# A recurrent cell and a gated feed-forward layer: the seven-product form of the up product from the third chunk on, with the second gate on GpSimd

## The chip, the cores and the metric

The kernel runs on one core of a Trainium2 chip. The time is device microseconds (us) of one execution. A core has a matrix engine (TensorE, PE in the profile, with its weight loads PEld), a vector engine (VectorE, DVE), a scalar engine for activations (ScalarE, ACT), GpSimd (POOL) and SyncE (SP), which here issues most transfers. Each engine works through its own queue in order and waits for others by semaphores. PE writes to PSUM, a memory of banks of 128 x 512 float32; GpSimd works in SBUF, the main on-chip memory.

## The reference

Two layers follow each other. The first is a recurrent cell with a matrix state C and a vector state n, for 4 batches of 8 heads, 768 steps, head dimension 40:

```python
for t in range(S):
    m_new = np.maximum(f_gate[:, :, t] + m, i_gate[:, :, t])
    f_stab = np.exp(f_gate[:, :, t] + m - m_new)
    i_stab = np.exp(i_gate[:, :, t] - m_new)
    m = m_new
    C = f_stab[:, :, None, None] * C + i_stab[:, :, None, None] * np.einsum('bhd,bhe->bhde', vt, kt)
    n = f_stab[:, :, None] * n + i_stab[:, :, None] * kt
    h_tilde = np.einsum('bhde,bhe->bhd', C, qt)
    denom = np.maximum(np.abs(nq), 1.0)          # nq = n . q
    y[:, :, t] = o * h_tilde / denom             # o = sigmoid(o_gate)
```

Its output is rearranged to x with 3072 rows of 320. The second layer is

```python
h = x @ w_in            # 320 -> 2048
g = h * np.cos(h)
return g @ w_out        # 2048 -> 320
```

## The kernel before, in words

**Chunks, cells, slots.** The 768 steps are cut into 6 chunks of 128 (NC). In a chunk, one *cell* per batch b computes the recurrence in its parallel form for 8 heads; cells are numbered n = 4 * chunk + b. The feed-forward layer runs one chunk behind: while the cells of chunk c + 1 are computed, the up product, the gate and the down product of chunk c are. The 2048 columns of w_in are taken in 8 *slots* of 256 (f2 = 0 to 7, two halves e of 128), two slots to a cell. So a chunk has 4 cells or 8 slots, and `both_parts(c, b)` writes out the order of one cell and its two slots by hand: all engines' queues are in the order of these calls. The last chunk's slots (c = 5) have no cell beside them.

**A slot.** `Up` multiplies the transposed x (`xT`, `xL`: all 4 batches side by side, 512 columns) by two column blocks of w_in into two PSUM banks (`pup`, a pool of two, so that the next slot needs both free). L724 is the part over 256 of the 320 dimensions, L718 the last 64. x was scaled by 1/(2 pi) when the cell was normalised, so that the cosine is taken as a sine of the distance to the nearest whole number: `near` (ACT, L732, the whole number), `rest` (DVE, L735, the remainder), `sin` (ACT, L740), `gate` (DVE, L744: product times 2 pi times sine) into `g`.

**Two fast products.** Both large products have a seven-product form (Strassen's, in Winograd's variant). The down product uses it from chunk 1 on: `weight_sums` makes sums of blocks of w_out once, `sums(c, k)` makes for each slot four sums of blocks of g on DVE (L880 to L883, 128x128) into a tile S and four on GpSimd (L885 to L888) into tiles D, S and g; `products` yields 12 products of 160 columns a slot (L992), which `down_slot` runs in quotas of 12 to 14, one slot behind; `late_products` runs the 16 that are left of a chunk in slot 1 of the next. `combine_first`, `combine` (slot 0 of the next chunk, L1002 and L1010 to L1020) and `combine_late` (slot 1, L1025 to L1027) add up the four accumulator banks into outputs.

The up product has the seven-product form in `UpFast`, in chunk 5 only (`fast = NC - 1`). `up_weight_sums` puts sums of w_in blocks into the tiles that held the cells' q and k, which are free by then; `x_sums` makes sums of x blocks. `UpFast` runs four products of 256 columns (L790), two ACT copies of the banks into a tile `s` (L798, L799), a filler of two down products (`fill_in`), three more products on top of what is in the banks, and the last dimensions (L806). Additions of parts of `s` follow on GpSimd (L807, L809) and DVE (L808), then on DVE into the bank b0 (L810) and of b1 and `s` into `s` (L812), which frees b1.

**A cell beside the slots.** In the first slot of a cell: `scores` (PE, L539), `weigh` (DVE, L545, needs the decays E), `decay_exponents` and `decay` of the next cell (GpSimd L423, ACT L437), `values` (PE, L565 to L574), `seam` (PE, L676), `normalize_turned` (DVE, L592 to L613), `fade` (GpSimd, L659). In the second: `seam_out` (a transfer of xL issued by ACT, L683), `state` (DVE, L701), `weigh_k` (GpSimd, L442), at its end `turn_blocks` of the next cell (two DVE transposes, L517) and `scale_q` (GpSimd, L521). `sin_next` loads ACT's table for the sine ahead of use (L1208). At the end of chunks 1 to 3, `sigmoid` (L343, L345) prepares the output gate of the chunk after the next.

The functions that the change touches, with the line numbers of the profile:

Of the kernel before, what the change touches and what calls it, by code (L numbers as in the profile page):

```python
# [11 lines left out]
FP = mybir.dt.float32  # L12
# [17 lines left out]
def kernel(  # L30
# [20 lines left out]
    nc = tc.nc  # L51
# [24 lines left out]
    pb = ctx.enter_context(tc.tile_pool(name="pb", bufs=4))  # L76
# [9 lines left out]
    nil = const.tile([128, 128], BF, name="nil")  # L86
# [4 lines left out]
    firsts = p2.tile([128, 4, C], FP, name="first", tag="S")  # L91
# [3 lines left out]
    wall = const.tile([128, HP, C], BF, name="wall")  # L95
# [3 lines left out]
    ident_b = const.tile([128, 128], BF, name="ident_b")  # L99
# [3 lines left out]
    ks2 = [const.tile([128, 2, H, 64], FP, name=f"ks{i}") for i in range(2)]  # L103
    vs2 = [const.tile([128, 2, H, DV], FP, name=f"vs{i}") for i in range(2)]
    for i in range(2):
        nc.gpsimd.memset(ks2[i][:, :, :, D:64], 0.0)
        nc.gpsimd.memset(vs2[i][:, :, :, D:DV], 1.0)
# [8 lines left out]
    WR = 2 * HP * (C // 32) * D  # L116
    raws = {w: [const.tile([128, WR + 32], FP, name=f"{w}r{i}") for i in range(2)] for w in "qk"}
    for w in "qk":
        nc.vector.memset(raws[w][0], 0.0)

    def clear_low():

        for w in "qk":
            for r in (slice(32, 64), slice(64, 128)):
                nc.scalar.copy(out=raws[w][1][r], in_=raws[w][0][r])


# [16 lines left out]
    def bits_in(n, src, pool, width):  # L144
        bits = pool.tile([128, width, 2], I32, name="bits", tag="bits")
        for rows, piece in src:
            nc.sync.dma_start(out=bits[rows, 0:n], in_=piece)
        return bits
# [44 lines left out]
    def weights_in(f):  # L193
        for i in range(NK):
            src = [(slice(32 * a, 32 * a + 32), w_in_bits[D * (NK * a + i):D * (NK * a + i) + 32, ts(f, WP)]) for a in range(HP)]
            yield w_in_sb[:, i, ts(f, WP)], bits_in(WP, src, pb, WP)
        bits = pb.tile([128, WP, 2], I32, name="bits", tag="bits")
        for e in range(2):
            for a in range(2):
                nc.sync.dma_start(out=bits[64 * e:64 * e + 64, ts(a, 128)].rearrange("r n two -> r (n two)"), in_=w_in_last[e, 2 * f + a])  # L200
        yield w_in_l[:, ts(f, 2)].rearrange("p a n -> p (a n)"), bits
# [18 lines left out]
    spare = [raws[w][1][0:BH, x:x + WQ] for w in "qk" for x in (0, WQ)]  # L220
    spare.append(pc.tile([128, 2 * WQ], FP, name="spare", tag="bits")[0:BH, 0:WQ])
# [89 lines left out]
    def ks(n):  # L311
        return ks2[n // 2 % 2][:, n % 2]
# [42 lines left out]
    def load_two(n, which="qkKv"):  # L355
        c, b = divmod(n, B)
        m = n // 2 % 2
        for name, src in (("q", q), ("k", k)):
            if name in which:
                src = src.rearrange("b (p j) (c t a) d -> j c t (b p) (a d)", j=2, a=C // 32, t=32)  # L360
                for j in range(2):
                    for low in range(1 if n < 2 * B else 2):
                        x = 0 if low else 32
                        dst = raws[name][m][64 * j + 32 * low:64 * j + 32 * low + 32, x:x + WR]
                        nc.sync.dma_start(out=dst.rearrange("t (p x) -> t p x", x=C // 32 * D),
                                          in_=src[j, c, :, 4 * b:4 * b + 8])
        for name, dst, src in (("K", ks2[m], k), ("v", vs2[m], v)):
            if name in which:
                src = src.rearrange("b h (c t) d -> c t b h d", t=C)
                nc.sync.dma_start(out=dst[:, :, :, 0:D], in_=src[c, :, b:b + 2])  # L370
# [14 lines left out]
    def load_M(n):  # L385
        c, b = divmod(n, B)
        if n == B - 1:
            E = pb.tile([128, H, C], FP, name="E3", tag="bits")
# [41 lines left out]
    def decay(n):  # L430
# [4 lines left out]
        for h in range(H):  # L435
# [3 lines left out]
    def weigh_k(n):  # L439
        if n < N - B:  # L440
            kw = p2.tile([128, H, 64], FP, name="kw", tag="kw")
            nc.gpsimd.tensor_tensor(out=kw, in0=ks(n), in1=cols(n, 1, 64), op=OP.mult)  # L442
# [27 lines left out]
    def load_blocks(n):  # L470

        c, b = divmod(n, B)
        m, x = n // 2 % 2, n % 2 * (WR // 2)
        for name, src in (("q", q), ("k", k)):
            src = src.rearrange("b (p j) (c t a) d -> j c t (b p) (a d)", j=2, a=C // 32, t=32)
            for j in range(2):
                dst = raws[name][m][64 * j:64 * j + 32, 32 + x:32 + x + WR // 2]
                nc.sync.dma_start(out=dst.rearrange("t (p x) -> t p x", x=C // 32 * D), in_=src[j, c, :, HP * b:HP * b + HP])

    def low_dimensions_of(n):  # L480
        x = 32 + n % 2 * (WR // 2)
        for w in "qk":
            for j in range(2):
                lo, hi = (raws[w][n // 2 % 2][64 * j + y:64 * j + y + 32, x:x + WR // 2].rearrange("t (x d) -> t x d", d=D) for y in (0, 32))
# [17 lines left out]
    def low_dimensions(n):  # L502

        for w in "qk":
            for j in range(2):
                lo, hi = (raws[w][n // 2 % 2][64 * j + x:64 * j + x + 32, 32:32 + WR].rearrange("t (x d) -> t x d", d=D) for x in (0, 32))
                nc.scalar.copy(out=hi[:, :, 0:D - 32], in_=lo[:, :, 32:D])

    def turn_blocks(n, which="qk"):
        m = n // 2 % 2  # L510
        if n not in qkT:
            qkT[n] = [p1.tile([128, HP, C], FP, name=f"t{i}", tag=f"t{i}") for i in range(2)]
        for w in which:
            i = "qk".index(w)
            x = 32 + n % 2 * (WR // 2)
            src = raws[w][m][:, x:x + WR // 2].rearrange("q (p a d) -> q p a d", a=C // 32, d=D)
# [103 lines left out]
    def normalize(n):  # L620
# [8 lines left out]
        t = p1.tile([128, 3 * C], FP, name="yo", tag="db")[:, 0:DM].rearrange("q (h d) -> q h d", h=H)  # L629
# [31 lines left out]
    def seam(n):  # L661
# [9 lines left out]
        if n < N - B:  # L671
            pu = pool.tile([128, HP, DV], FP, name="pu", tag=tag)
            for p in range(HP):
                for j in range(2):
                    h = 2 * p + j
                    nc.tensor.matmul(pu[64 * j:64 * j + D, p], kws[n][:, h, 0:D], vs(n)[:, h], start=True, stop=True)  # L676
# [29 lines left out]
    class Up:  # L706
# [35 lines left out]
        def gate(self, e):  # L742
            g = gp.tile([128, B * C], FP, name="g", tag="g")
            nc.vector.scalar_tensor_tensor(out=g, in0=self.pu[e], scalar=TWO_PI, in1=self.n[e].bitcast(FP),  # L744
                                           op0=OP.mult, op1=OP.mult)
# [5 lines left out]
    fast = NC - 1  # L751
    Sw, Tx = {}, {}

    def up_weight_sums(part):

        tt = nc.gpsimd.tensor_tensor
        if part == 0:
            S1, S2, S4, S3 = Sw.setdefault(0, [raws[w][m][:, 0:NF // 2 * 128].rearrange("p (f n) -> p f n", n=128)
                                               for m in range(2) for w in "qk"])
            tt(out=S1, in0=A21, in1=A22, op=OP.add)  # L760
            tt(out=S2, in0=S1, in1=A11, op=OP.subtract)
        else:
            S1, S2, S4, S3 = Sw[0]
            tt(out=S3, in0=A11, in1=A21, op=OP.subtract)
            tt(out=S4, in0=A12, in1=S2, op=OP.subtract)

# [4 lines left out]
    def x_sums(c):  # L771
        T1, T2, T4 = Tx[c] = pe.tile([128, H, C], FP, name="Tx", tag="E")[:, 0:3 * B // 2].rearrange("p (k b) t -> k p b t", k=3)
# [6 lines left out]
    class UpFast(Up):  # L779


        def __init__(self, c, f2, fill):
# [14 lines left out]
            s = pe.tile([128, H, C], FP, name="Sx", tag="E").rearrange("p (k b) t -> p k (b t)", k=4)  # L797
# [10 lines left out]
            nc.vector.tensor_tensor(out=s[:, 0], in0=s[:, 0], in1=s[:, 3], op=OP.add)  # L808
            nc.gpsimd.tensor_tensor(out=s[:, 3], in0=s[:, 1], in1=s[:, 2], op=OP.add)  # L809
            nc.vector.tensor_tensor(out=b0[:, second], in0=b0[:, second], in1=s[:, 0], op=OP.add)  # L810
            h = s[:, 0:4:3]
            nc.vector.tensor_tensor(out=h, in0=b1.rearrange("p (k n) -> p k n", k=2), in1=h, op=OP.add)  # L812
            self.n = [p3.tile([128, B * C], I32, name="n", tag="n") for _ in range(2)]
            self.h = h

        def near(self, e):
            if e == 0:
                return super().near(e)
# [606 lines left out]
```

## Time and profile before

The median of three runs is 524.11 us (523.25 to 526.92). The profiled execution took 525.5 us.

| | profiled execution |
|---|---|
| time | 525.5 us |
| span of the trace | 523.7 us |
| granted PE clock | 1.000 |
| bytes moved | 57.83 MB, mean 110 GB/s |
| matrix products of the up product, full form (L724) | 146.4 us busy, 320 records of 600 ns |
| its last dimensions (L718) | 45.2 us, 160 records of 641 ns |
| the same in seven products (L790, L806; chunk 5) | 32 + 5 x 16 records of 379 to 389 ns, 32 of 641 ns |
| down products (L992) with S, D, g | 58.4 + 55.1 + 35.4 + 28.7 + 23.6 us |
| waits of GpSimd for gates (L885 <- L744) | 145.2 us in 30 waits |

Times in the profile are us from the span's start unless marked ns; a busy share counts time in which an engine executed, and waiting does not count. A float32 matrix product appears as two records, so `x8` stands for four products. Records of consecutive products overlap, so the mean of a record is longer than the distance of two. The stages are: to 42 us the first four cells and the first weights; from 42 to some 131 us chunk 0's slots with the weights arriving; then chunk 1 to 207.3, chunk 2 to 287.4, chunk 3 to 367.4, chunk 4 to 446.0, chunk 5 to about 514, and the last outputs.

### The profile page before, as it was taken

To read this page: it belongs to the slowest core of one execution; us is meant where nothing else is said; L and a number is where in the kernel's file an instruction comes from. 1 tells how busy PE (TensorE), PEld (TensorE's weight loads), DVE (VectorE), ACT (ScalarE), POOL (GpSimd) and SP (SyncE) were. 2 spreads that over 40 slices of the span, in tenths; PEclk is the share of its full clock that TensorE was granted. 3 is DMA by queue.
4 is the path that set the end of the run, shared out by engine and by line. 5 is a ranking of instruction groups with operands and counts; after the bars stand their busy time and mean duration, and the time that the engine had idled before them with its cause. 6 is when DMAs were issued, how large, how long until landed. Compare 5 with 4: busy or idle time off the path is not lost.

```text
span 523.7 us, 10589 instructions
## 1 busy us (share of the span) xinstructions
PE 504.7 (96%) x3894; PEld 353.0 (67%) x3894; DVE 415.3 (79%) x852; ACT 301.2 (58%) x570; POOL 247.3 (47%) x392
## 2 busy tenths in 40 slices
PE   6999897979999999999999999999999999999996
PEld 4874564545567676676677677667667767787876
DVE  5899998686868878898778888868898868787875
ACT  6899896647656547744537736526836522343541
POOL 7534654442875753543543642642425435435341
PEclk9999999999999999999999999999999999999999
DMA  9989979898849159149159239159220000010001
GB/s 138 211 221 231 260 162 220 179 187 210 166 143 190 56 114 165 41 122 171 52 115 157 51 100 176 44 118 165 42 81 6 2 5 7 2 50 1 1 1 51
DMA packets 100196, 57.83 MB, mean 110 GB/s; under 512 B 62432, under 2 KB 92736, under 8 KB 100144
## 3 DMA queue, kind: packets, MB, share of 16 engines
q1 hardware_dynamic: 96608, 55.48, 49.1%
q10 hardware_dynamic: 3392, 1.49, 1.4%
q8 instruction: 31, 0.51, 0.4%
q14 instruction: 21, 0.17, 0.1%
q0 software_dynamic: 144, 0.18, 0.1%
HBM read 51.71 MB, written 4.11 MB: 107 GB/s over the span
## 4 chain that ended last, share of the span: by engine, by line
PE 67%; DMA 10%; ACT 6%; SPq 5%; DVE 5%; POOL 4%; issue 2%; ACTq 0%; DVEq 0%; POOLq 0%
PE acc L992 24%; PE pup L724 19%; PE pup L718 6%; PE pup L790 5%; PE late L992 3%; DMA xL<-xT 3%; PE ps L539 3%; ACT E L437 2%; PE vt L574 2%; DMA bits<-in_moe_w_in_dram 2%; PE vt L565 2%; PE pup L806 2%; DMA bits<-in_moe_w_out_dram 2%; SPq L353 1%; DMA E<-M_d 1%
## 5 line engine op out<-in xcount | busy, mean ns | idle before, releaser
L724 PE MATMUL pup<-xT,w_in_sb 128*128 128x512 f32 x320 | 146.4, 600 | 3.8 <-DVE g L744 3.6
L732 ACT ACTIVATE n<-pup 128x512 int32<-128x512 f32 x88 | 49.7, 593 | 156.5 <-PE pup L718 87.9
L724 PEld LDWEIGHTS pup<-xT,w_in_sb 128*128 128x128 f32 x320 | 57.7, 189 | 78.6 <-issue 77.0
L885 POOL TENSOR_TENSOR D<-g 128x128 f32<-128x128 f32 x40 | 20.1, 501 | 177.4 <-DVE g L744 145.2
L735 DVE SCALAR_TENSOR_TENSOR n<-pup,n 128x512 f32<-128x512 f32 x88 | 58.1, 687 | 56.2 <-ACT n L732 54.9
L740 ACT ACTIVATE n<-n 128x512 f32<-128x512 f32 x96 | 58.1, 628 | 20.6 <-DVE n L735 11.2
L744 DVE SCALAR_TENSOR_TENSOR g<-pup,n 128x512 f32<-128x512 f32 x88 | 56.8, 684 | 2.6 <-ACT n L740 1.9
L992 PE MATMUL acc<-w_out_sb,g 128*128 128x160 f32 x320 | 58.4, 303 | 0.0
L992 PE MATMUL acc<-T,g 128*128 128x160 f32 x304 | 55.1, 300 | 0.2 <-DVE g L883 0.2
L437 ACT ACTIVATE E<-E,tab 128x128 f32<-128x128 f32 x160 | 49.0, 388 | 4.2 <-POOL E L423 4.0
L992 PEld LDWEIGHTS acc<-w_out_sb,g 128*128 128x128 f32 x320 | 48.1, 190 | 4.4 <-issue 2.7
L718 PE MATMUL pup<-xL,w_in_l 64*128 64x512 f32 x160 | 45.2, 641 | 3.6 <-POOL w_in_l L179 3.6
L992 PEld LDWEIGHTS acc<-T,g 128*128 128x128 f32 x304 | 45.8, 190 | 2.3 <-issue 1.4
L843 PE MATMUL po<-w_out_sb,g 128*128 128x320 f32 x128 | 36.3, 436 | 2.6 <-POOL w_out_sb L179 2.6
L992 PE MATMUL acc<-T,S 128*128 128x160 f32 x160 | 35.4, 303 | 0.0
L843 PEld LDWEIGHTS po<-w_out_sb,g 128*128 128x128 f32 x128 | 23.9, 190 | 14.3 <-POOL w_out_sb L179 3.6
L539 PEld LDWEIGHTS ps<-t,t 40*128 40x128 f32 (+1 forms) x384 | 24.8, 188 | 10.3 <-issue 5.4
L545 DVE TENSOR_TENSOR E<-ps,E 128x512 f32<-128x512 f32 x48 | 30.7, 680 | 0.0
L992 PEld LDWEIGHTS acc<-T,S 128*128 128x128 f32 x160 | 26.1, 190 | 6.0 <-issue 6.0
L992 PE MATMUL acc<-w_out_sb,S 128*128 128x160 f32 x160 | 28.7, 299 | 0.0
L179 POOL TENSOR_TENSOR w_out_sb<-w_out_sb,bits 128x640 int32<-128x640 int32 x8 | 12.6, 1573 | 32.8 <-ACT E L437 14.4
L521 POOL TENSOR_TENSOR qG<-t,G 128x512 f32<-128x512 f32 x20 | 25.4, 1271 | 4.4 <-DVE t L517 4.2
(232 smaller groups left out, 981.4 us busy)
## 6 DMA issues: line engine op xcount, KB each, us to landing
E<-M_d SPq DMA_DIRECT2D x22, 512.0 KB, 3.6
qr<-in_q_dram SPq DMA_DIRECT2D x34, 160.0 KB, 3.2
kr<-in_k_dram SPq DMA_DIRECT2D x34, 160.0 KB, 5.0
bits<-in_moe_w_out_dram SPq DMA_DIRECT2D x8, 640.0 KB, 4.0
G<-G_d SPq DMA_DIRECT2D x18, 256.0 KB
bits<-in_moe_w_in_dram SPq DMA_DIRECT2D x32, 128.0 KB, 4.6
out_dram<-o_sb SPq DMA_DIRECT2D x23, 160.0 KB, 1.9
o<-in_o_gate_dram SPq DMA_DIRECT2D x40, 80.0 KB, 3.2
```

The source lines that it names most:

```text
L437: nc.scalar.activation(out=Es[n][:, h], in_=Es[n][:, h], func=AF.Exp, scale=-1.0, bias=tab[:, c, 0, g:g + 1])
L539: nc.tensor.matmul(ps[j][:, p], kT[r, p], qT[r, p], start=True, stop=True)
L545: nc.vector.tensor_tensor(out=w, in0=pss[n][j], in1=w, op=OP.mult)
L718: nc.tensor.matmul(pu, w_in_l[r, f2], xL[c][r].rearrange("p b t -> p (b t)"), start=ahead, stop=not ahead)
L724: nc.tensor.matmul(pu.rearrange("p (b t) -> p b t", b=B), w_in_sb[:, i, ts(2 * f2 + e, 128)], xT[c][:, i:NK * B:NK], start=(i == 0 and not ...
L732: nc.scalar.activation(out=self.n[e], in_=self.pu[e], func=AF.Copy, bias=0.25)
L735: nc.vector.scalar_tensor_tensor(out=self.n[e].bitcast(FP), in0=self.pu[e], scalar=0.25, in1=self.n[e], op0=OP.add, op1=OP.subtract)
L740: nc.scalar.activation(out=r, in_=r, func=AF.Sin, scale=TWO_PI_DOWN)
L744: nc.vector.scalar_tensor_tensor(out=g, in0=self.pu[e], scalar=TWO_PI, in1=self.n[e].bitcast(FP), op0=OP.mult, op1=OP.mult)
L790: nc.tensor.matmul(bank[:, part].rearrange("p (b t) -> p b t", b=B // 2), w[:, f2], x, start=start, stop=stop, skip_group_check=True)
L843: nc.tensor.matmul(po[c][b], gs[c, f][:, ts(b, C)], w_out_sb[:, f], start=(f == 0), stop=(f == NF - 1))
L992: nc.tensor.matmul(a, lhs, rhs, start=start, stop=stop)
```

## The change

1. `fast` is 2: chunks 2 to 5 use `UpFast`. A new `both_parts_fast` writes out the order of a cell and two slots for them. The decays of the next cell are split: six heads after the sines of the first slot, two (`range(AHEAD, H)`) in the second slot after its copies. `scale_q` moves from the end of the second slot to the start of the next cell; `sums` of the second slot moves behind `turn_blocks`; `seam` becomes the filler of the second slot, and the two down products stay the filler of the first.
2. The second gate (e = 1) of a fast slot goes to GpSimd, whose product has no scalar factor, as does the addition of L808; b1 is added up into `g` itself and freed.
3. The factor 2 pi leaves the gates and is applied when outputs are added up (`add_turns`, and a scale of ACT's copies).
4. `sums` becomes four DVE operations of 128x256 and none on GpSimd, in all chunks.
5. Memory: q and k blocks are loaded a cell at a time (`load_blocks`) into two half-size buffers; one tile `blocks` holds rings for S, D, the weights' bits and `s`; the sums of w_in lie in a tile `room` whose space the first cells' k uses before, and in place of one w_in block. They are made in chunk 1, by three calls in place of two. The copies on ACT that cleared the second q and k buffers at the start are gone.

```diff
-    fast = NC - 1
+    fast = 2
...
-            s = pe.tile([128, H, C], FP, name="Sx", tag="E").rearrange("p (k b) t -> p k (b t)", k=4)
+            s = blocks[:, FREE_AT:FREE_AT + 8].rearrange("p (k b) t -> p k (b t)", k=4)
...
             nc.gpsimd.tensor_tensor(out=s[:, 1], in0=s[:, 1], in1=s[:, 0], op=OP.add)
-            nc.vector.tensor_tensor(out=s[:, 0], in0=s[:, 0], in1=s[:, 3], op=OP.add)
+            nc.gpsimd.tensor_tensor(out=s[:, 0], in0=s[:, 0], in1=s[:, 3], op=OP.add)
             nc.gpsimd.tensor_tensor(out=s[:, 3], in0=s[:, 1], in1=s[:, 2], op=OP.add)
             nc.vector.tensor_tensor(out=b0[:, second], in0=b0[:, second], in1=s[:, 0], op=OP.add)
-            h = s[:, 0:4:3]
-            nc.vector.tensor_tensor(out=h, in0=b1.rearrange("p (k n) -> p k n", k=2), in1=h, op=OP.add)
+            self.g = gp.tile([128, B * C], FP, name="g", tag="g")
+            nc.vector.tensor_tensor(out=self.g.rearrange("p (k n) -> p k n", k=2), in0=b1.rearrange("p (k n) -> p k n", k=2), in1=s[:, 0:4:3], op=OP.add)
...
+            tt = nc.vector.tensor_tensor if (self.c, self.f2) == (NC - 1, NF // 2 - 1) else nc.gpsimd.tensor_tensor
+            tt(out=self.g, in0=self.g, in1=self.n[e].bitcast(FP), op=OP.mult)
...
+    def add_turns(out, in0, in1):
+
+        nc.vector.scalar_tensor_tensor(out=out, in0=in0, scalar=TWO_PI, in1=in1, op0=OP.mult, op1=OP.add)
...
+        tt(out=S2_D1, in0=G0[:, :, 1], in1=G1[:, :, 1], op=OP.add)
+        tt(out=G0[:, :, 1], in0=G0[:, :, 0], in1=G0[:, :, 1], op=OP.subtract)
+        tt(out=S0_S1, in0=S2_D1, in1=G0[:, :, 0], op=OP.subtract)
+        tt(out=S3_D4, in0=G1[:, :, 0], in1=S0_S1, op=OP.subtract)
...
+    def filled(c, f2):
+
+        return c >= fast and (f2 != 1 if c >= NC - 2 else f2 % 2 == 0)
...
     def fill_in(c, f2):
+        if filled(c, f2):
+            run(products_of(c if f2 > 0 else c - 1), FILL)
+        elif (c + 1) * B + f2 // 2 < N:
+            seam((c + 1) * B + f2 // 2)
...
+    def both_parts_fast(c, b):
+
+        n = (c + 1) * B + b
+        cell, follows = n < N, n + 1 < N
+        for i in range(2):
+            f2 = 2 * b + i
+            up = UpFast(c, f2, lambda: fill_in(c, f2))
+            if cell and i == 0:
+                scores(n)
+                scale_q(n)
+            if cell and i == 1:
+                if follows:
+                    decay(n + 1, range(AHEAD, H))
+                    sin_next()
+                if n % 2 == 1 and n + 3 < N:
+                    load_two(n + 3)
+                if b == B - 1:
+                    x_sums(c + 1)
+            for e in range(2):
+                up.near(e)
+            for e in range(2):
+                up.rest(e)
+            if cell and i == 0:
+                weigh(n)
+                if follows:
+                    decay_exponents(n + 1)
+            if cell and i == 1:
+                seam_out(n)
+                state(n)
+                if follows:
+                    weigh_k(n + 1)
+                    odd_values(n + 1)
+            for e in range(2):
+                up.sin(e)
+                up.gate(e)
+            if i == 0:
+                if follows:
+                    decay(n + 1, range(AHEAD))
+                sums(c, f2)
+            if i == 1 and b == B - 1 and c < NC - 2:
+                sigmoid(c + 2)
+                sin_next()
+            down_slot(c, f2)
+            if f2 == 0:
+                for p in range(2):
+                    combine_first(c - 1, p)
+            if cell and i == 0:
+                values(n)
+                normalize_turned(n)
+                fade(n)
...
+            if f2 == 0:
+                for p in range(2):
+                    combine(c - 1, p)
+            if i == 1:
+                if follows:
+                    turn_blocks(n + 1)
+                sums(c, f2)
```

## The prediction

> **What bounds the kernel now.** I read the page first, its busy shares:
>
> ```profile
> PE 504.7 (96%) x3894; PEld 353.0 (67%) x3894; DVE 415.3 (79%) x852; ACT 301.2 (58%) x570; POOL 247.3 (47%) x392
> ```
>
> PE is nearly full and DVE next. Shares average over stages, so then the stretches of one cell's two slots (chunk 3) and of five slots of the last chunk. The columns are the stretch, its length, busy time (instructions) of PE, PEld, DVE, ACT, POOL, the granted clock, DMA share, GB/s:
>
> ```profile
> 327.39:347.41 20.02, 20.02 (x169) 14.13 (x169) 15.45 (x33) 9.88 (x19) 8.69 (x17) 1.00 0.29 74
> 463.20:503.60 40.40, 40.40 (x231) 33.15 (x231) 31.05 (x60) 18.01 (x31) 16.56 (x30) 1.00 0.03 9
> ```
>
> PE has no gap in either, at full clock. The chain that ended last (start, length, what) gives the price of both forms of the up product on PE:
>
> ```profile
> 327.39 3.43 PE pup L724 x8
> 330.82 1.06 PE pup L718 x4
> 331.88 0.89 PE ps L539 x16
> 332.77 4.00 PE acc L992 x28
> ...
> 463.20 1.73 PE pup L790 x8
> 465.47 1.29 PE pup L790 x6
> 466.76 1.06 PE pup L806 x4
> ```
>
> The full product is 3.43, the seven-product form 1.73 + 1.29 = 3.02, with a filler of 0.54 (two down products, not extra work) between its parts; 1.06 for the last dimensions is in both.
>
> **The change, part by part.** I call a cell's first slot even, its second odd, T a slot's start on PE and L the end of its last-dimension products.
>
> *PE.* Chunks 2, 3 and 4 take the short form: 24 slots x 0.41 = -9.8. Chunk 5 has it already. A cell then takes 20.02 - 0.82 = 19.2, if nothing is late.
>
> *ScalarE, and the queue at a chunk's end.* Each fast slot puts two copies (L798, L799: 0.59 each) between the first four products and the rest: the fifth product waits for the first copy. In slot 7 of a chunk the next-but-one chunk's sigmoids stand behind the sines on ACT, and the copies of the next slot stand behind them. The timeline of ACT there, before:
>
> ```profile
> 364.89 1.15 ACT L740 ACTIVATE n<-n 128x512 f32<-128x512 f32 x2 [0.64 <-issue]
> 366.06 1.28 ACT L343 ACT_TABLE_LOAD   x1
> 367.35 1.06 ACT L343 ACTIVATE og<-o 128x1024 f32<-128x1024 f32 x1
> 368.31 0.51 ACT L345 ACTIVATE og<-o 128x128 f32<-128x128 f32 x2
> 368.84 1.28 ACT L1208 ACT_TABLE_LOAD   x1
> 370.13 0.20 ACT L1208 ACTIVATE spot<-spot 1x1 f32<-1x1 f32 x1
> ```
>
> From the sine's end to the spot's end is 4.3; today ACT's next work is due only at 371.94. After a fast slot 7 the sine ends at T-0.2 (below), so the copies run from T+4.1 and the fifth product starts at T+4.7 and not at T+2.27: 2.5 lost before chunks 3 and 4 with the sixth product's wait. Before chunk 2, slot 7 is still the full product, the sine ends at T-1.4 as here (366.04 against 367.42), and 1.4 is lost; under that lies a 0.75 wait of the second product for GpSimd's new sums of x. Together +6.4. ScalarE: Activation LUTs of the Trainium skill (What ACT_TABLE_LOAD costs) adds a drain of about 1.38 to each switch of set. The trace disagrees: the sigmoid starts 0.01 after its load ends. By that page the three boundaries would cost an estimated 3 x 2 x 1.38 = 8.3 more (538.8 in all), which I leave out.
>
> *VectorE and GpSimd in a fast slot with a cell.* From the last chunk's rows: addition into b0 0.43 (L810), into b1 0.69 (L812), two remainders 0.69, gate 0.69; the second gate leaves for GpSimd at 1.27 (L521, also 128x512) and three additions stay there or come, 0.72 each (L807, L809). The sums are four VectorE operations of 256 (0.43, L808), not four of 128 there (0.28 to 0.50) and four on GpSimd. What matters is who meets whom:
>
> ```profile
> 394.44 2.36 POOL L761 TENSOR_TENSOR kr<-qr,w_in_sb 128x1024 f32<-128x1024 f32 x1
> ...
> 395.99 0.95 DVE L880 TENSOR_TENSOR S<-g 128x128 f32<-128x128 f32 x1
> ...
> 396.75 1.14 POOL L423 TENSOR_SCALAR_AFFINE_SELECT E<-E 128x1024 f32<-128x1024 f32 x1
> ...
> 396.98 1.06 DVE L881 TENSOR_TENSOR S<-S,g 128x128 f32<-128x128 f32 x1
> ```
>
> A VectorE operation with both inputs in SBUF, 0.29 alone, ends 0.15 after the GpSimd operation that it met, and GpSimd's next gets in first: one sum for each GpSimd operation. PSUM-fed operations (L735, L744) keep 0.69 beside GpSimd. SBUF — State Buffer of the Trainium skill (Who interferes with whom) has this as an exclusive lock for a whole instruction; the trace agrees, and it speaks against moving work to GpSimd.
>
> Walk of a cell without extra work. Odd slot: in the last chunk the gate starts 2.66 after L (470.48 - 467.82); four state additions (0.86, L701) lie ahead of it here, so it ends at L+4.2, the sine at L+3.8. PE starts the next slot at L+4.0 and needs that bank at L+4.9: clear. Two transposes (L517, start 0.95 apart, 1.1 each) end at L+6.2, which is T+2.1; then the sums. GpSimd's three additions begin at T+2.4 (second copy's end) and alternate with them: the sums end at T+5.5, not T+3.7, and the next slot's addition into b0, due at T+4.65, is 0.9 late. The second remainder (now both inputs in SBUF) then meets the affine select (1.1): both weighings end at T+9.7, where PE wants the second half of E at T+9.4: 0.36 per cell. Four such cells (two each in chunks 2 and 3): +1.4. Bounds: 0 if the sums get in first, 1.4 each if they fall one operation later and meet qG (1.27) too. In chunk 4 there is no state addition, the sums are 0.86 earlier: 0.
>
> *Slots 0 to 2 of a chunk.* There VectorE also adds up the last chunk's outputs:
>
> ```profile
> 381.04 0.48 DVE L1010 TENSOR_TENSOR o_sb<-acc,o_sb 128x320 f32<-128x320 f32 x1
> ...
> 383.79 0.32 DVE L1020 TENSOR_TENSOR o_sb<-acc,o_sb 128x160 f32<-128x160 f32 x1
> 384.03 1.28 DVE L735 SCALAR_TENSOR_TENSOR n<-pup,n 128x512 f32<-128x512 f32 x2
> ...
> 390.47 1.07 DVE L517 STREAM_TRANSPOSE t<-kr 128x512 f32<-128x512 f32 x1
> ```
>
> That is 3.07, and it pushes the remainders; the transposes end at 391.54 and PE's scores begin at 391.60: no slack is left today. After: in slot 0 the sums wait for GpSimd's gate (sine + 1.3), then follow normalisation (3.1: L592 378.00 to L613 381.12) and the 3.07, ending about 20.8 after the slot's start with the sigmoid's delay in it. Slot 1's L comes at 18.0, so its addition is 2.8 late, its gate ends at 25.0, and slot 2's third product, due at 23.65, waits 1.4; the late products wait 0.4 for a bank. That is 1.8 in chunks 2 and 3, 0.9 in chunk 4. Slot 2's sums then fall behind the additions and meet qG and the affine select: between 0.3 (additions only) and 2.7; 2.2, because in the rows above two sums did cost two long GpSimd operations. Chunks 2 and 3 only. Sum 1.8 + 1.8 + 0.9 + 2.2 + 2.2 = +8.9.
>
> *Tail.* After the last gate the four sums took 2.1 under GpSimd's (512.45 to 514.56); alone four of 0.43 start 0.34 apart: -0.5.
>
> *At nothing.* Clearing copies off ACT (L125, four of 1.28): the chain of the first 46 us runs over GpSimd memsets, the M_d transfer and SP's issues, not ACT; at most -2. 19 more SP issues (about 0.5 each) and the same bytes: DMA share is 0.3 to 0.8 here; if they were late, +1. Weight sums moved into chunk 1 (four L760 lengths, 9.5): GpSimd is idle for 24 of the 57 us from 150 on and loses its half of the sums. The 2 pi in L1010 and its kin: scaled (L744) and plain (L812) forms cost 0.69 alike. Slot 1 of chunk 4 has no filler (+0.5), slot 0 of chunk 5 gets one (-0.5).
>
> Sum: -9.8 + 6.4 + 1.4 + 8.9 - 0.5 = +6.4. The profiled execution took 525.5 (span 523.7), 1.4 above the median 524.1 of the runs; on the median, 530.5.
>
> **Rivals.** *Queues clear (faster):* VectorE is 15.5 of 20.0 busy and gains 0.9 a cell, so it could fit 19.2; all waits vanish but part of the sigmoid's: -9.8 to -5.5, so 514 to 518.6. Against it: ACT works in order, and that stall needs no contention. It decides if the copies are not held by more than about 1.4 at a boundary. *Boundary only:* the sums get in before the additions and the output sums hide: -9.8 + 6.4 - 0.5 = -3.9, 520; with half of the 8.9, 524.6. For it: sums start 0.3 ahead of the additions in the walk. *VectorE behind in every cell:* the four cells at 1.4 and not 0.36 (+4.2), slot 2 at 2.7 and chunk 4 as late as the others (+1 and +3): 537 to 540. For it: normalisation ends within 0.1 of the next addition's due time, so a small delay carries on. *Not doing what it says:* the instruction listing has seven products in all slots of chunks 2 to 5; no chance.
>
> **Numbers.** Forecast (527 to 535) 0.44; VectorE behind 0.14; boundary only, to 527, 0.27; queues clear 0.15. A measurement here tells about 1% (5.2) from no change: under 518.9 faster 0.16, to 529.3 same 0.34, slower 0.50. The range leaves out half of the clear case and the top of the worst: 517 to 539.
>
> **What would show it.** Right: ACT copies after the spot at three boundaries with PE idle 1.4 to 2.5; PE waiting for the gate in slot 2; sums of 0.7 and more beside GpSimd's additions, a cell at 19.5 to 20. Wrong: cells at 19.2 throughout, slot 2 included, or PE idle in the first 150 us.

## The result, and the profile after

The changed kernel takes 531.25 us (median of four runs, 530.71 to 531.94) against 524.62 (523.25 to 526.92): a ratio of 1.0116, 95% interval 1.0088 to 1.0145. Its profiled execution spans 529.6 us, 5.9 more than before. The page's busy shares after:

```profile
PE 504.2 (95%) x4038; PEld 377.6 (71%) x4038; DVE 433.4 (82%) x863; ACT 326.3 (62%) x617; POOL 280.8 (53%) x355
```

PE's records are busy for 0.5 less than before (504.7), with some 1.6 in it that a halved clock added (last section), so the short form bought little there in sum, and all other engines have more to do. The stretches after, with the columns of the prediction's second fence (length, busy PE, PEld, DVE, ACT, POOL, granted clock, DMA, GB/s): a steady stretch of one cell's length (the odd slot of chunk 3's third cell and the even slot of its fourth), and the first and the second cell's slots of chunk 3.

```profile
343.14:362.75 19.61, 19.61 (x184) 16.16 (x180) 17.72 (x35) 12.44 (x24) 11.63 (x15) 1.00 0.39 99
287.53:311.25 23.72, 21.57 (x182) 16.94 (x181) 18.08 (x40) 15.90 (x30) 12.18 (x17) 0.93 0.25 71
311.25:332.39 21.14, 20.11 (x182) 16.02 (x181) 19.96 (x41) 13.05 (x25) 12.43 (x17) 1.00 0.61 131
```

Steady cells fell from 20.02 to 19.61 with PE full. The first two cells of a chunk are 4.1 and 1.5 longer than that, with 2.2 and 1.0 of PE idle and, in the first, a granted clock of 0.93. PE's waits after (us in total, times, longest):

```profile
PE pup L783 <- ACT blocks L791: 6.3, 4, 2.2
...
PE vt L556 <- DVE E L536: 2.2, 3, 0.7
...
PE pup L783 <- DVE g L735: 1.6, 3, 0.9
```

Of the 6.3, 6.0 is the fifth product waiting for the first copy (L791) at the starts of chunks 2, 3 and 4: 1.70, 2.15 and 2.19. The other two lines are waits in slot 2 of each of these chunks: of the values (L556) 0.74 each, of the third product for the gate 0.85, 0.29 and 0.51. ACT's timeline at chunk 3's start, in answer to the one of before:

```profile
286.05 1.29 ACT L731 ACTIVATE n<-n 128x512 f32<-128x512 f32 x2 [0.54 <-DVE n L726]
287.36 1.28 ACT L352 ACT_TABLE_LOAD   x1
288.65 1.06 ACT L352 ACTIVATE og<-o 128x1024 f32<-128x1024 f32 x1
289.61 0.51 ACT L354 ACTIVATE og<-o 128x128 f32<-128x128 f32 x2
290.14 1.28 ACT L1192 ACT_TABLE_LOAD   x1
291.44 0.20 ACT L1192 ACTIVATE spot<-spot 1x1 f32<-1x1 f32 x1
291.55 0.56 ACT L791 COPY blocks<-pup 128x512 f32<-128x512 f32 x1
```

From the sines' end (287.34) to the spot's end it is 4.3 again, and the copy starts at T + 4.0 (T = 287.53). As before, the sigmoid starts 0.01 after its table load ends (288.65 against 287.36 + 1.28): no drain of the kind that ScalarE: Activation LUTs of the Trainium skill (What ACT_TABLE_LOAD costs) adds.

The timeline of slot 2 in chunk 3, in answer to the rows in which VectorE and GpSimd met:

```profile
315.02 0.51 DVE L863 TENSOR_TENSOR blocks<-g 128x256 f32<-128x256 f32 x1
315.32 0.79 POOL L801 TENSOR_TENSOR blocks<-blocks 128x256 f32<-128x256 f32 x1
...
315.56 0.83 DVE L864 TENSOR_TENSOR g<-g 128x256 f32<-128x256 f32 x1
...
316.19 0.79 POOL L802 TENSOR_TENSOR blocks<-blocks 128x256 f32<-128x256 f32 x1
316.32 0.94 DVE L865 TENSOR_TENSOR blocks<-blocks,g 128x256 f32<-128x256 f32 x1
...
316.94 1.45 POOL L512 TENSOR_TENSOR qG<-t,G 128x512 f32<-128x512 f32 x1
317.29 1.38 DVE L866 TENSOR_TENSOR blocks<-g,blocks 128x256 f32<-128x256 f32 x1
...
318.60 0.42 DVE L803 TENSOR_TENSOR pup<-pup,blocks 128x256 f32<-128x256 f32 x1
```

The second to fourth sum each end 0.28 after the GpSimd operation that they met (316.39 against 316.11, 317.26 against 316.98, 318.67 against 318.39), one for one, and the addition into the bank (L803), due when PE finished the last dimensions at 316.4, starts at 318.60.

In a steady cell the same operations come in time (VectorE and GpSimd in a slot that starts at 352.00):

```profile
353.99 0.41 DVE L863 TENSOR_TENSOR blocks<-g 128x256 f32<-128x256 f32 x1
...
354.71 0.74 POOL L800 TENSOR_TENSOR blocks<-blocks 128x256 f32<-128x256 f32 x1 [1.68 <-ACT blocks L792]
354.78 0.94 DVE L865 TENSOR_TENSOR blocks<-blocks,g 128x256 f32<-128x256 f32 x1
...
355.76 0.83 DVE L866 TENSOR_TENSOR blocks<-g,blocks 128x256 f32<-128x256 f32 x1
...
356.94 0.43 DVE L803 TENSOR_TENSOR pup<-pup,blocks 128x256 f32<-128x256 f32 x1 [0.35 <-PE pup L799]
```

Only two of the four sums are stretched beside GpSimd's additions, the last ends at 356.59, and the addition into the bank waits 0.35 for PE.

Where the 5.9 lie, by the slots' starts: 2.6 gained before chunk 2, then chunk 2 +2.9 (82.96 against 80.06), chunk 3 +4.0, chunk 4 +2.1, chunk 5 up to its last slot +0.1, the end 0.7 gained.

### The profile page after: what moved, and what is told of

The parts are those of the page before. It is cut to its first block, busy times and chain, and to the rows that moved or that the text cites. A ratio compares the mean times of both kernels' runs of the same rounds, so it can differ in the third digit from the quotient of the medians.

```text
span 529.6 us, 11051 instructions
## 1 busy us (share of the span) xinstructions
PE 504.2 (95%) x4038; PEld 377.6 (71%) x4038; DVE 433.4 (82%) x863; ACT 326.3 (62%) x617; POOL 280.8 (53%) x355
## 3 DMA queue, kind: packets, MB, share of 16 engines
q10 hardware_dynamic: 3392, 1.49, 1.2%
## 4 chain that ended last, share of the span: by engine, by line
PE 59%; DVE 13%; DMA 9%; ACT 7%; SPq 5%; POOL 4%; issue 3%; ACTq 0%; DVEq 0%; POOLq 0%
PE acc L975 18%; PE pup L783 14%; PE pup L715 7%; PE pup L799 5%; PE po L824 3%; DVE n L726 3%; DMA ks<-in_k_dram 2%; PE pup L709 2%; PE ps L530 2%; DVE o_sb L836 2%; PE late L975 2%; DMA G<-G_d 2%; PE vt L565 2%; PE vt L556 2%; ACT n L723 2%
## 5 line engine op out<-in xcount | busy, mean ns | idle before, releaser
L723 ACT ACTIVATE n<-pup 128x512 int32<-128x512 f32 x64 | 36.8, 593 | 121.3 <-DVE pup L803 84.3
L813 POOL TENSOR_TENSOR g<-g,n 128x512 f32<-128x512 f32 x31 | 39.6, 1277 | 75.0 <-ACT n L731 75.0
L726 DVE SCALAR_TENSOR_TENSOR n<-pup,n 128x512 f32<-128x512 f32 x64 | 43.1, 689 | 22.0 <-ACT n L723 19.3
L715 PE MATMUL pup<-xT,w_in_sb 128*128 128x512 f32 x128 | 58.8, 602 | 2.0 <-DVE g L735 1.8
L800 POOL TENSOR_TENSOR blocks<-blocks 128x256 f32<-128x256 f32 x32 | 25.3, 790 | 57.7 <-ACT blocks L792 57.7
L783 PE MATMUL pup<-xT,w_in_sb 128*128 128x256 f32 x192 | 53.8, 386 | 1.8 <-DVE g L735 1.6
L735 DVE TENSOR_TENSOR g<-pup,n 128x512 f32<-128x512 f32 x64 | 42.5, 685 | 2.4 <-ACT n L731 1.7
L783 PE MATMUL pup<-x_room,room 128*128 128x256 f32 x128 | 39.3, 389 | 0.0
L803 DVE TENSOR_TENSOR pup<-pup,blocks 128x256 f32<-128x256 f32 x32 | 13.7, 430 | 29.5 <-PE pup L799 26.9
L975 PE MATMUL acc<-T,blocks 128*128 128x160 f32 x160 | 36.3, 309 | 0.0
```

Source lines behind the costliest of these rows:

```text
L715: nc.tensor.matmul(pu.rearrange("p (b t) -> p b t", b=B), w_in_sb[:, i, ts(2 * f2 + e, 128)], xT[c][:, i:NK * B:NK], start=(i == 0 and not ...
L723: nc.scalar.activation(out=self.n[e], in_=self.pu[e], func=AF.Copy, bias=0.25)
L726: nc.vector.scalar_tensor_tensor(out=self.n[e].bitcast(FP), in0=self.pu[e], scalar=0.25, in1=self.n[e], op0=OP.add, op1=OP.subtract)
L735: nc.vector.tensor_tensor(out=g, in0=self.pu[e], in1=self.n[e].bitcast(FP), op=OP.mult)
L783: nc.tensor.matmul(bank[:, part].rearrange("p (b t) -> p b t", b=B // 2), w[:, f2], x, start=start, stop=stop, skip_group_check=True)
L813: tt(out=self.g, in0=self.g, in1=self.n[e].bitcast(FP), op=OP.mult)
```

## The experiments

Slot lengths are distances between first products on PE. Times are medians; ratios are to the kernel before on the same chip. The third cell is slots 4 and 5.

| kernel | us | ratio, 95% interval | slots 0, 1, 2 of chunk 3 | third cell there |
|---|---|---|---|---|
| before | 524.6 | | 11.08, 8.94, 11.62 | 20.02 |
| changed | 531.25 | 1.0116, 1.0088 to 1.0145 | 14.33, 9.39, 12.29 | 19.61 |
| e1_last_only | 522.58 | 0.9945, 0.9926 to 0.9965 | 11.07, 8.94, 11.87 | 20.02 |
| e2_late_sigmoid | 525.75 | 1.0013, 0.9991 to 1.0035 | 10.71, 10.38, 12.91 | 19.61 |
| e3_sums_first | 536.54 | 1.0209, 1.0178 to 1.024 | 12.77, 9.77, 13.04 | 19.82 |
| e4_filler_odd | 533.26 | 1.0148, 1.0111 to 1.0185 | 13.90, 9.31, 13.33 | 19.47 |
| g1_gate_vector | 539.55 | 1.0274, 1.0236 to 1.0312 | 12.75, 9.91, 14.08 | 19.75 |
| x1_outputs_later | 528.87 | 1.0067, 1.0035 to 1.0099 | 10.69, 10.38, 13.10 | 19.61 |
| x2_sums_later | 521.59 | 0.9932, 0.991 to 0.9954 | 10.69, 10.36, 10.77 | 19.75 |
| x3_filler_state | 528.92 | 1.0076, 1.0047 to 1.0105 | 12.38, 10.26, 11.78 | 20.53 |
| x5_slots_0_1 | 519.45 | 0.991, 0.9879 to 0.994 | 10.70, 9.40, 11.64 | 19.61 |
| s1_order_alone | 526.28 | 1.0025, 1.0007 to 1.0044 | 12.74, 9.78, 10.75 | 19.73 |

**The rest of the change without its first part.**

```diff
-    fast = 2
+    fast = 5
```

> Everything of the change but its first part: the seven-product slots stay in chunk 5 alone, as before. Theory: the new memory layout and the sums on VectorE gained 2.6 us ahead of chunk 2 and 0.7 us behind the last gate, and all that was lost lies in chunks 2 to 4. Then this takes 524.6 - 2.6 - 0.7 = 521.3 us (519.5 to 522.5), less than both kernels, and cells of 20.0 in chunks 2 and 3. Rival: the layout, the sums on VectorE or the loads by cell cost time in every cell; then chunks 2 and 3 take more than 80.1 each and the whole is 524 or more.

522.58 us: the theory's direction, 1.3 more than its centre and just outside its range. Chunk 2 starts at 204.97 (before 207.13, changed 204.57), the distance from the last slot to the end is 0.7 shorter (19.6 against 20.3), and chunks 2 to 4 take 80.32, 80.31 and 78.18 against 80.06, 80.07 and 78.59. The rival's sign for chunks 2 and 3, more than 80.1 each, came by 0.25 a chunk, in slot 2 (11.87 against 11.62); its total did not. So layout, loads by cell and sums on VectorE gain as a whole, and the loss is that of the short form in chunks 2 to 4, with the order of work that comes with it.

**The sigmoid moved off the chunk's end.**

```diff
-            if i == 1 and b == B - 1 and c < NC - 2:
-                sigmoid(c + 2)
-                sin_next()
...
             up = UpFast(c, f2, lambda: fill_in(c, f2))
+            if f2 == 0 and c + 1 < NC:
+                sigmoid(c + 1)
```

(The same three lines go from `both_parts` for chunk 1.)

> The sigmoids of the next-but-one chunk no longer stand behind the sines of a chunk's last slot but behind the copies of the next chunk's first slot, for chunks 2 to 4. Theory: the fifth product then waits at none of the three chunk starts (2.2 us each today), and the granted clock, which fell to half for 3.4 us behind that wait at chunk 3's start, stays at 1.0 (1.7 us); some 3 us come back as a later sine and later VectorE work in slot 0: 526 us (524 to 528). Rival: VectorE's addition of the outputs is what is late in slots 0 to 2, and the stall only covers it; then 529.5 to 531.5, with longer waits for the gate in slots 1 and 2. Second rival, for the clock: it falls without the wait too, for another reason.

525.75, as the theory said. The two copies now run at once and the sigmoids behind them (ACT's timeline at chunk 3's start, which is 285.00 here):

```profile
286.12 0.59 ACT L791 COPY blocks<-pup 128x512 f32<-128x512 f32 x1 [1.29 <-PE pup L783]
286.99 0.59 ACT L792 COPY blocks<-pup 128x512 f32<-128x512 f32 x1 [0.28 <-PE pup L783]
287.59 1.28 ACT L352 ACT_TABLE_LOAD   x1
```

Slot 0 shrank from 14.33 to 10.71, while slots 1 and 2 grew from 9.39 and 12.29 to 10.38 and 12.91: the sine comes 1.3 later behind a second table load, and VectorE's queue, not yet mended, shows more of itself. The clock stayed at 1.00 from 200 us to the last product of this execution, which speaks against the second rival; the last section has more on it.

**Sums ahead of the transposes.**

```diff
+                sums(c, f2)
                 if follows:
                     turn_blocks(n + 1)
-                sums(c, f2)
```

> In the second slot of a cell the four sums stand ahead of the two transposes instead of behind them, so that they meet fewer of GpSimd's additions. Theory (sums and GpSimd's operations take turns): the sums in slot 2 of chunks 2 and 3 take 1.7 us and not 3.5, and the second cells there shrink by about 1 us each; 529.2 us. Rival: those cells are late because the addition of the outputs is, not because of the sums; then no change (531), or 1 to 3 us more, since the transposes now end 1.7 later and the scores wait for them.

536.54: the rival, and more than it allowed. The scores, which waited for nothing in the changed kernel, now wait for the transposes:

```profile
PE ps L530 <- DVE t L508: 4.7, 5, 1.1
```

Slot 2 did not shrink either (13.04 against 12.29, 0.9 of it that wait): in both places tried within the slot, what stands behind the sums pays for them.

**Down products as filler in the odd slots.**

```diff
-        return c >= fast and (f2 != 1 if c >= NC - 2 else f2 % 2 == 0)
+        return c >= fast and f2 != 1
...
-        elif (c + 1) * B + f2 // 2 < N:
-            seam((c + 1) * B + f2 // 2)
...
                 values(n)
+                seam(n)
                 normalize_turned(n)
```

> In chunks 2 and 3 the filler between the two parts of the seven-product form is two down products in the odd slots too (slot 1 has none), and the products of the state's increment stand behind the values in the even slot, as in the kernel before. Theory: the odd slot saves nothing because products of another shape stand in its middle and each change of shape shows about 0.2 us of weight load; then steady cells take 19.4 and not 19.6, 1 us over six cells: 530.2. Rival: the cell is set by VectorE's or GpSimd's turn, and then it stays at 19.6 (531.2), with a wait of PE in it.

The mechanism held and the total did not: the third and fourth cells of chunk 3 are 19.47 and 19.51, and the kernel takes 533.26 against 530.2. PE's timeline of one odd slot, first in the kernel before, where it starts with the last dimensions:

```profile
338.84 1.13 PE L718 MATMUL pup<-xL,w_in_l 64*128 64x512 f32 x4
339.90 3.70 PE L724 MATMUL pup<-xT,w_in_sb 128*128 128x512 f32 x8
343.44 0.43 PE L992 MATMUL acc<-w_out_sb,S 128*128 128x160 f32 x2
343.71 0.71 PE L992 MATMUL acc<-w_out_sb,g 128*128 128x160 f32 x4
...
347.24 0.59 PE L724 MATMUL pup<-xT,w_in_sb 128*128 128x512 f32 x1
```

then in the changed kernel:

```profile
343.14 0.70 PE L783 MATMUL pup<-x_room,room 128*128 128x256 f32 x2
...
345.07 0.54 PE L667 MATMUL pu<-vs,kw 128*40 128x48 f32 x16
345.54 0.70 PE L783 MATMUL pup<-x_room,w_in_sb 128*128 128x256 f32 x2
...
347.03 1.13 PE L799 MATMUL pup<-xL,w_in_l 64*128 64x512 f32 x4
348.09 0.54 PE L975 MATMUL acc<-w_out_sb,blocks 128*128 128x160 f32 x2
348.47 0.71 PE L975 MATMUL acc<-w_out_sb,g 128*128 128x160 f32 x4
...
352.00 0.38 PE L783 MATMUL pup<-x_room,room 128*128 128x256 f32 x1
```

and with the other filler:

```profile
343.86 0.70 PE L783 MATMUL pup<-x_room,room 128*128 128x256 f32 x2
...
345.69 0.43 PE L975 MATMUL acc<-w_out_sb,blocks 128*128 128x160 f32 x2
345.96 0.43 PE L975 MATMUL acc<-w_out_sb,g 128*128 128x160 f32 x2
346.23 0.59 PE L783 MATMUL pup<-x_room,w_in_sb 128*128 128x256 f32 x2
...
347.64 1.13 PE L799 MATMUL pup<-xL,w_in_l 64*128 64x512 f32 x4
...
352.07 0.38 PE L783 MATMUL pup<-x_room,room 128*128 128x256 f32 x1
```

Read by starts, without filler: the odd slot's up products took 3.54 before (339.90 to 343.44), take 1.93 + 1.49 in the changed kernel and 1.83 + 1.41 here; an even slot's take 1.73 + 1.41. The first two down products take 0.38 behind the last dimensions (348.09 to 348.47), where they took 0.27 behind the up product before (343.44 to 343.71). So each change of shape goes with about 0.1, half of what was expected: two around the filler, which this kernel gets back (0.18), one in the slot's first four products (1.83 against 1.73), one in the first down products. Together they are the 0.38 that the even slot saves and the odd one does not; whether weight loads are the reason is not shown. Chunk 4 of the changed kernel, where no state's increment is needed and odd slots have down products as filler, agrees: 8.40 before, 8.21 after. What ate the gain: the odd slot is 0.65 shorter, VectorE's gate is not, and the third product's waits for it rose from 1.6 to 3.0 in all. The profile also had the clock drop described at the end, in chunk 4.

**The second gate back on VectorE.**

```diff
-            tt = nc.vector.tensor_tensor if (self.c, self.f2) == (NC - 1, NF // 2 - 1) else nc.gpsimd.tensor_tensor
-            tt(out=self.g, in0=self.g, in1=self.n[e].bitcast(FP), op=OP.mult)
+            nc.vector.tensor_tensor(out=self.g, in0=self.g, in1=self.n[e].bitcast(FP), op=OP.mult)
```

> The changed kernel with the second gate of every fast slot back on VectorE (product of two SBUF tiles there, 0.7 us, in place of 1.27 on GpSimd). Theory: what is late in slots 0 to 2 is VectorE's queue, so 0.7 more per slot there pushes the transposes and the next additions: slots 1 and 2 grow by 0.5 to 1.5 us together in each of chunks 2 to 4, 532 to 535 us, while the steady cell stays at 19.6. Rival: the sums are late because they wait for GpSimd's gate and then take turns with GpSimd; then the sums start earlier and the kernel takes 528 to 530.

539.55: the theory's side, beyond its 535. Slot 2 grew by 1.3 to 1.8 in each chunk, the waits of the values for E rose from 2.2 to 6.8 in all, and chunk 4's steady even slots took 11.73 in place of 10.76, though the theory had left steady cells alone. In this order of work GpSimd was the right place for the gate.

**Outputs added up behind slot 1's gate,** on top of the late sigmoid; then, in the next run, **slot 1's sums in slot 2** as well.

```diff
             if f2 == 0:
-                for p in range(2):
-                    combine(c - 1, p)
+                combine(c - 1, 0, (0,))
...
+            if f2 == 1:
+                combine(c - 1, 0, (1,))
+                combine(c - 1, 1)
             down_slot(c, f2)
```

(`combine` has got a third argument: part 0 is its first addition, part 1 the rest.)

> The late sigmoid, and of the eight VectorE operations that add up the last chunk's outputs in slot 0 only the first (which frees a bank for the late products) stays there; seven move behind the gate of slot 1. Theory: they stood ahead of slot 1's additions and gate and so made slot 2's third product wait 0.9 us; that wait goes in all three chunks and slot 1 shrinks by 0.3 to 1: 523 us (522 to 524.5) against 525.75 for the late sigmoid alone. Rival: VectorE has too much to do in slots 0 to 2 in whatever order, and the transposes of slot 1, now behind all seven, make slot 2's scores wait as long: 525 to 527.

528.87: a miss for both. The third product's wait is gone, but slot 1's transposes and sums stand behind the seven operations and fall fully into GpSimd's operations. VectorE's timeline in chunk 2's slot 2:

```profile
230.96 0.83 DVE L864 TENSOR_TENSOR g<-g 128x256 f32<-128x256 f32 x1
231.72 1.49 DVE L865 TENSOR_TENSOR blocks<-blocks,g 128x256 f32<-128x256 f32 x1
233.24 1.19 DVE L866 TENSOR_TENSOR blocks<-g,blocks 128x256 f32<-128x256 f32 x1
234.35 0.42 DVE L803 TENSOR_TENSOR pup<-pup,blocks 128x256 f32<-128x256 f32 x1
```

The values then wait 2.1 for E in all three chunks. Of seven executions, six show a mean clock of 0.990 to 0.997 and take 528.2 to 530.3; one shows 1.000 and takes 525.9, inside the rival's 525 to 527.

```diff
+            if f2 == 2:
+                sums(c, 1)
...
                     turn_blocks(n + 1)
-                sums(c, f2)
+                if f2 > 1:
+                    sums(c, f2)
```

> As the kernel with outputs added up later, and the four sums of slot 1 (first needed in slot 3) move from the end of slot 1 to slot 2, behind that slot's own sums. Theory: ahead of slot 2's addition into the bank they took turns with GpSimd's additions for 3.5 us and made the values wait 0.7 us for the second half of E; that wait goes in chunks 2 and 3: 521.5 us (520.5 to 523). Rival: they then delay the normalisation and with it slot 3's addition, and the wait only moves to slot 4: 523.

521.59, as the theory said. With no sums in the way, the same stretch of chunk 3 runs without a stretched addition:

```profile
308.20 1.10 DVE L508 STREAM_TRANSPOSE t<-kr 128x512 f32<-128x512 f32 x1
309.74 0.43 DVE L803 TENSOR_TENSOR pup<-pup,blocks 128x256 f32<-128x256 f32 x1 [0.45 <-PE pup L799]
```

VectorE now waits 0.45 for PE, and slot 2 is 10.77, a steady even slot. The rival is half right: slot 4, next in line, is 0.6 longer in chunk 2 (11.36) and 0.13 in chunk 3, and in chunk 5, where the sums moved too, slot 3 waits 0.87 for them. Both moves on the changed kernel, with the sigmoid left where it was:

> The changed kernel with the sigmoids left at the chunk ends, and only VectorE's order changed: outputs added up behind the gate of slot 1, slot 1's sums in slot 2. It completes a table of four with the changed kernel (531.25), the late sigmoid (525.75) and both together (521.6). Theory: the stall on ScalarE at a chunk's start and VectorE's late queue in slots 0 to 2 are two separate losses, so the order alone is worth 4.2 here as well: 527.1 us (526 to 528.3), with the fifth product's waits of 1.7 to 2.2 still there and slot 2 at 10.8. Rival: VectorE is late because the stall delays it, and without the stall gone the order helps little: 529.5 to 531. Second rival: the stall gives VectorE time that the new order uses, and both moves together count twice: 525 or less.

526.28, the theory. The four kernels make a table: VectorE's order is worth 5.0 with the sigmoid at the chunk's end (531.25 to 526.28) and 4.2 with it moved (525.75 to 521.59); the sigmoid's place is worth 5.5 and 4.7. Within the intervals, about 1 us each, the two losses are separate; the sigmoid's share includes the halved clock of some executions (last section).

**Filler and state's additions, on top of x2.** Besides the filler of e4:

```diff
-                state(n)
...
                 up.gate(e)
+            if cell and i == 1:
+                state(n)
```

> As the kernel with both moves, and in addition two down products as filler in the odd slots of chunks 2 and 3 with the state's products behind the values, and the state's additions on VectorE behind the gate and not ahead of it, so that the gate ends 0.8 us earlier. Theory: the odd slot then takes 8.2 and the even one 11.2, a cell 19.44 in place of 19.61, and the earlier gate keeps the third product of the even slot from waiting as it did with the filler alone: 520.3 us. Rival: the transposes, which now end later against an earlier slot, or the gate are late all the same, and it takes 521.5 to 524.

528.92, worse than both. The slot's transposes now stand behind the state's additions and end 3.3 after the next slot's start (331.12 in a slot that begins at 327.85), where the walk of the prediction had 2.1. So in steady cells too the sums (330.97 to 334.72) meet three additions, qG and each other's turns, the addition into the bank comes at 334.74 where PE was done at 332.6, and the values wait 0.87 for E. Even slots take 12.32. This is the prediction's third rival, VectorE behind in every cell, made by two small moves: in e4, with the odd slot 0.65 shorter and the state's additions in their old place, the transposes of chunk 3's third cell end 2.7 after its slot's start, its bank addition starts at 5.5, and its even slot takes 11.26, 0.47 of it the state's products; here it is 3.3, 6.9 and 12.32.

**Slots 0 and 1, on top of x2.**

```diff
-                    decay(n + 1, range(AHEAD))
+                    decay(n + 1, range(4 if b == 0 else AHEAD))
...
-                for p in range(2):
-                    combine_first(c - 1, p)
+                combine_first(c - 1, 0)
+                combine(c - 1, 0, (0,))
...
             if f2 == 1:
+                combine_first(c - 1, 1)
...
-            if f2 == 2:
+            if f2 == 2 and c < NC - 1:
                 sums(c, 1)
```

(The decays left over and chunk 5's sums follow suit.)

> As the kernel with the late sigmoid, the outputs added up later and slot 1's sums later, and four small moves more: in slot 0 only four decays stand ahead of slot 1's copies and not six; the scaling copy for the second pair of outputs goes from slot 0 to slot 1; the one addition of outputs left in slot 0 stands ahead of the normalisation; and chunk 5 keeps its own order of sums. Theory: what is left in slots 0 and 1 are waits for the first copy (0.5, 0.5 and 1.0), for the late products' bank (0.3 twice) and 0.9 in chunk 5, and all go: 521.6 - 3.4 = 518.2 us (517.3 to 519.5). Rival: the decays moved into slot 1 push its sines and the gate, and slot 2's third product waits: 520 to 522.

519.45: inside the theory's range at its upper end, and the fastest kernel here. The waits for the first copy and the late bank are gone but for 0.2, and so is chunk 5's 0.9. Part of it came back: the scores of slot 2 now wait 0.6 for the transposes in chunks 2 and 3, and in chunk 3 slots 0 to 2 together are only 0.1 shorter than in x2. Against e1 the short form from the third chunk on is then worth 0.4% by the two ratios and 0.7% by the profiled spans (517.2 against 520.9); the two intervals just overlap, so its sign is likely and not settled.

## The prediction, point by point

Predicted 530.5, measured 531.25. The two losses that decide the sign were named rightly. That the number came so close is luck: the short form's gain was 4.2 too large and 1.6 of halved clock was not foreseen, while the start, slots 0 to 2 and the steady cells' wait came out 2.6, 1.9 and 1.4 better than said.

- *Short form on PE, -9.8.* Mis-sized: -5.6. Eight cells fell by 0.41 and chunk 4's four by 0.58, not all by 0.82. The even slot saves 0.38, as the price from chunk 5 said. The odd slot saves nothing: its up, last-dimension and down products took 8.40 before and take 8.39. The step that failed, "24 slots x 0.41", took the even slot's price for both, though in the odd one products of other shapes stand in the middle and on both sides of the up products, four changes of about 0.1. With down products in the middle, e4 got 0.14 a cell back.
- *Sigmoid ahead of the copies, +6.4.* Right: 6.0 of PE idle (1.70, 2.15, 2.19 against 1.4, 2.5, 2.5). e2 and the pair s1 and x2 show it. The 0.75 wait for sums of x shows neither at chunk 2's start nor in e2, where no stall covers it. Not foreseen: the halved clock behind one of these gaps, +1.6 in the profiled execution (slot 0 of chunk 3 took 14.33, and 12.77 in e3 with the same wait and no drop).
- *Steady cells' wait, +1.4.* Wrong: PE waits for nothing in a steady cell. The walk had the sums meet three GpSimd additions and end at T+5.5; they met two, as GpSimd began at T+2.7 and not T+2.4, and ended at T+4.6, before PE was done. That is the walk's own lower bound. That the cell still came out at 19.61 beside the 19.56 forecast is chance, one error hiding the other.
- *Slots 0 to 2, +8.9.* Right in kind, over in size. The first two cells of chunks 2 to 4 exceed steady ones by 15.0; less 0.4 that chunk 4's did before, 6.0 of stall and 1.6 of clock, 7.0 are left. The third product's waits for the gate were smaller than said (1.6 in three waits). Slot 2's sums met GpSimd's additions and qG as walked through (3.66 from 315.02 to 318.67), but the values waited 0.74 for it and not 2.2, and in chunk 4 as well, which the walk left out. The orders of s1 and x2 took 5.0 and 4.2 of the 7.0 away. All waits in these slots but the stall come to 4.5; the other 2.5 is time in which PE shows busy, and no run takes it apart.
- *Start, at nothing, at most -2.* Mis-sized: -2.6. PE's waits of the full form shrank, for a gate from 3.6 to 1.8, for w_out's conversion from 2.6 to 1.7, for the last dimensions' weights from 3.6 to 2.9; by the slots' starts, 1.1 is lost ahead of chunk 0's first slot (other kernels with this layout start it 1.2 earlier to 1.6 later), 2.9 gained in chunk 0 and 0.8 in chunk 1. Between 40 and 131 us the q and k transfers moved 1.9 MB in place of 3.2, and the main DMA queue's share was 79.0% in place of 86.9%, though all it moved fell only from 18.4 to 18.0 MB: the loads by cell may be the cause, but no run isolates them.
- *Tail, -0.5:* -0.7.
- *Rivals.* "Queues clear" and "boundary only" asked for slots 1 and 2 on time; they were not. "VectorE behind in every cell" asked for waits in steady cells; there are none.

## What to carry to other kernels

A product's price is taken from the slot it will stand in, with the products before and after it: changes of tile shape, here about 0.1 us each, can cost what the shorter form saves. Where work gets a step between its parts on another engine (here ACT's copies), that engine's queue must be read at every place where something long stands ahead, such as a table load. Work with slack, like sums that are needed a slot later, belongs behind the operations that gate the critical engine, above all when it takes turns with GpSimd: in the changed kernel a sum took 0.41 alone and 0.83 to 1.38 beside it.

## What the hardware showed unexpectedly

The granted PE clock fell to half for 3.4 us behind a gap of 2.15 us. PE's timeline of the changed kernel at chunk 3's start, and the stretches around it (length, then busy times; the clock is third from the end):

```profile
292.16 0.70 PE L783 MATMUL pup<-x_room,w_in_sb 128*128 128x256 f32 x2 [2.15 <-ACT blocks L791]
...
293.18 1.06 PE L783 MATMUL pup<-xT,room 128*128 128x256 f32 x2
294.16 2.08 PE L799 MATMUL pup<-xL,w_in_l 64*128 64x512 f32 x4
```

```profile
292.16:293.15 0.99, 0.99 (x4) 0.78 (x5) 0.00 (x0) 0.42 (x1) 0.49 (x1) 1.00 0.66 180
293.15:296.57 3.42, 3.42 (x13) 1.71 (x13) 0.20 (x1) 0.00 (x0) 3.26 (x5) 0.50 0.16 45
```

The last dimensions take 1.87 from start to start there (294.16 to 296.03) and 0.96 to 1.06 elsewhere. After 200 us and up to the last products, the profiles of all kernels here have 16 gaps of 2.0 to 2.3 on PE; four were followed by such a drop, 0.1 to 1.4 us after work had resumed. Six gaps of 1.3 to 1.75 were not, and no drop stands there without such a gap. TensorE: Matmul & The Clock Gate of the Trainium skill (What's actually happening) has a free-running window of 3413 ns by whose activity the clock is set: the drop's length agrees, and so does that the same gap sometimes passes. It speaks of a whole idle window before the clock is lowered; here gaps of two thirds of one were enough. So a wait of 2 us can cost some 1.6 more (14.33 against 12.77 above), by chance. The mean clocks of all executions fit, though they do not tell where a clock fell (x1's trace has a drop at 24 us too): 30 of 40 of the six kernels with such gaps show 0.997 or less, 4 of 49 of e1, e2, x2, x3 and x5, and 12 of 70 of the kernel before. Of s1's twelve, five show 0.993 to 0.997 and take 526.4 to 527.8, seven show 1.000 and take 524.5 to 526.8.
